# Building the attention diagonal from transposed r*k, with ScalarE, in the lead and the first block

## The chip, the core and the metric

One core of one Trainium2 chip runs the whole program. The metric is device microseconds (us) of one launch; the figure for a kernel is the median of its runs. Engines are named as in the profile: PE (TensorE matmul), PEld (its weight load), DVE (VectorE), ACT (ScalarE), POOL (GpSimd), SP (SyncE, which issues nearly all DMAs).

## The reference

```python
for t in range(768):                       # B=4, H=8, D=48, S=768
    cur = einsum('bhd,bhe->bhde', u * k[t], v[t])
    y[t] = einsum('bhd,bhde->bhe', r[t], state + cur)
    state = w * state + einsum('bhd,bhe->bhde', k[t], v[t])
x = y as (3072 tokens, 384)
h = x @ w_in;  x = (relu(h) ** 2) @ w_out         # layer 1, 384 -> 2048 -> 384
h = x @ w_in2; x = (h - tanh(h)) @ w_out2         # layer 2
```

A token's own term is a diagonal: (sum over d of r*u*k) times v. All other terms go through decays that are powers of w.

## The kernel before, in words

**Tiles.** 128 tokens of one batch are a tile `i`; tiles 0 to 3 are the first 128 tokens of the four batches, 4 to 7 the next 128, up to 23. Four tiles are a block `j` of 512 tokens. Each of the two dense layers runs as 16 units `f` per block: `gemm1` (9 matmuls of 512 columns, the products of high and low parts), an activation, `gemm2` (9 more).

**Lead.** The attention of tiles 0 to 3 stands before everything else, in `lead_*`. `rk` holds r and k with d on the partitions ("transposed"), `nat` holds r, k and v with tokens on the partitions ("natural"). `table_b` makes the powers of w by doubling (`vtab`, then `tk` and `tr`). `lead_a` multiplies transposed k and r by them, `lead_b` makes 128x128 scores on PE (`sc`). The diagonal comes from natural r: `lead_u` multiplies by u (POOL), `lead_r` by natural k, `lead_s` sums over d (DVE), `lead_d` spreads it over identity matrices `am`, half of them by POOL and half by ACT, and `lead_m` copies the scores of earlier tokens over them (DVE, four COPY_PREDICATED). `lead_k` decays natural k on POOL, with a table that `table_c` made by PE transposes. `lead_c` then makes y and the state on PE, and `lead_e` evacuates y as a high part (ACT) and a low part (DVE), and the state (ACT). `fill` puts dummy matmuls between, on PE.

**Later tiles** go through `att_*` in two halves of 64 tokens, while the dense units of the block before run. Tiles 4 to 7 run in units 0 to 11 of block 0 (called the first block here). `att_u`, `att_r`, `att_k` and both halves of `att_d` run on POOL, `att_s` (a sum), `att_a` (decays of r and k), `att_m` (predicated copy) and `decay` on DVE; `att_b`, `att_v`, `att_c` are PE matmuls; `put_state` copies the state into `vs` on ACT.

**Weights.** In the first block each unit's weights arrive as one 768 KB DMA into one of three buffers `raw` and are split: `conv0` (ACT), `conv1` (two DVE operations), `conv2` (ACT), `conv3` (POOL for units 0 to 2, DVE after), three units ahead of their matmuls. Then `raw` is free for the next DMA.

**Order.** The order is written out by hand at the end of the kernel: each engine runs its instructions in the order in which the calls stand there. A unit `n` of the first block runs `act1_low(n)`, `conv2` and `conv3(n+2)`, `front(n+1)` (its `gemm1` and activation), `conv1(n+3)`, any attention part, `gemm2_1(n)`, `conv0(n+4)`. One call sets the state of a tile's first half:

```python
def state_0(i):
    if TPB <= i < NTAU:
        s = st_m[i % TPB]
        put_state(i, 0, s)                 # ACT
        dec_t[i] = a2.tile([GP, NP, D], F32, tag="dec", name="dec")
        decay(dec_t[i], s)                 # DVE
```

Of the kernel before, what the change touches and what calls it, by code (L numbers as in the profile page):

```python
# [25 lines left out]
def decay_attention_moe_moe_kernel(  # L26
# [171 lines left out]
    def table_a():  # L198
        nc.sync.dma_start(out=vtab[:, :, 0], in_=w)

    def table_b():
# [18 lines left out]
        nc.vector.tensor_copy(tr[:, :, 0:64], tk[:, :, 127:63:-1])  # L220

    def table_c():
        kh = gp.tile([GP, NP, C], F32, tag="g", name="kh")
        nc.vector.tensor_tensor(
            kh[:, :, 0:127],
            vtab[:, :, 126::-1],
            vtab[:, :, 31:32].to_broadcast([GP, NP, 127]),
            op=ALU.mult,
        )
        nc.vector.tensor_copy(kh[:, :, 127:128], vtab[:, :, 31:32])  # L230
        pt = bank(7, "pt")
        for p in range(NP):
# [776 lines left out]
```

## Time and profile before

| | us |
|---|---|
| median of three runs | 926.96 |
| lowest and highest run | 926.81 and 927.23 |
| span of the profiled execution | 926.0 |
| PE busy | 896.6 (97%) |
| DVE busy | 638.8 (69%) |
| ACT busy | 631.8 (68%) |
| POOL busy | 255.1 (28%) |

The span runs from the first to the last instruction of the profiled execution; its own run time is not given apart, and the median is 0.96 us above its span. The lead takes the first 36 us, the first block ends at about 140 us, block 1 at about 223, layer 2 begins at about 530 and fills the rest. Busy shares over the whole span say little about the first 140 us, where the limits are others.

### The profile page before, as it was taken

Reading aid. Unit: us, or ns where it says so; the run is one execution under the profiler, and the core shown is the slowest. Engines: PE = TensorE matmul, PEld = TensorE weight load, DVE = VectorE, ACT = ScalarE, POOL = GpSimd, SP = SyncE. Lnnn points to the kernel's source line nnn. Section 1 sums busy time; section 2 is a strip of 40 time slices with the busy share of each in tenths; the row PEclk is TensorE's granted clock in tenths of the full one; section 3 lists DMA queues with packets and bytes.
Section 4 is the critical chain, followed back from the end, with each engine's and each line's share of the span. In section 5 each row is a group of like instructions: output and inputs, shape, how many; then the busy total and the mean of one; then the engine's idle time right before and its main releaser. Section 6 shows DMA issues by size and latency. Waiting matters only on the chain.

```text
span 926.0 us, 14869 instructions
## 1 busy us (share of the span) xinstructions
PE 896.6 (97%) x5688; PEld 731.8 (79%) x5688; DVE 638.8 (69%) x1016; ACT 631.8 (68%) x1121; POOL 255.1 (28%) x214
## 2 busy tenths in 40 slices
PE   6799989999999999999999999999999999999997
PEld 5687777887888788788888778888888888888885
DVE  8899971332242233123167799999999999999996
ACT  2756754444444444444588898888988988988985
POOL 4854423553555455453202011001001001010000
PEclk7989999999999999999999999999999999999999
DMA  8846711322131122210455100010100100100000
GB/s 234 223 151 196 221 55 43 92 55 81 52 99 51 56 79 56 79 53 8 176 199 210 65 27 12 7 52 11 57 8 6 57 12 1 57 12 1 34 1 35
DMA packets 32168, 67.73 MB, mean 73 GB/s; under 512 B 5600, under 2 KB 17888, under 8 KB 32096
## 3 DMA queue, kind: packets, MB, share of 16 engines
q1 hardware_dynamic: 31792, 66.48, 23.3%
q8 instruction: 45, 0.74, 0.3%
q10 hardware_dynamic: 304, 0.30, 0.2%
q14 instruction: 27, 0.22, 0.1%
HBM read 55.35 MB, written 9.44 MB: 70 GB/s over the span
## 4 chain that ended last, share of the span: by engine, by line
PE 83%; DVE 8%; ACT 4%; DMA 3%; issue 1%; SPq 0%; POOL 0%; ACTq 0%; DVEq 0%; POOLq 0%
PE h L579 37%; PE o L729 20%; PE acc L619 18%; PE y L413 2%; PE sc L351 2%; PE pv L362 2%; DVE ra L322 1%; DMA first_kv<-in_nat_dram 1%; DMA x2d<-x2s 1%; DVE w L107 1%; DMA raw<-in_w_dram 1%; DVE raw L92 1%; DVE raw L93 1%; DVE ra L372 1%; ACT x2s L635 1%
## 5 line engine op out<-in xcount | busy, mean ns | idle before, releaser
L579 PE MATMUL h<-xt,w 128*128 128x512 f32 x864 | 214.5, 394 | 0.0
L579 PE MATMUL h<-xs,w 128*128 128x512 f32 x864 | 211.4, 389 | 0.0
L579 PEld LDWEIGHTS h<-xt,w 128*128 128x128 f32 x864 | 164.6, 191 | 34.9
L579 PEld LDWEIGHTS h<-xs,w 128*128 128x128 f32 x864 | 162.2, 188 | 34.0
L593 ACT ACTIVATE g<-h 128x512 f32<-128x512 f32 x96 | 57.2, 596 | 153.9 <-PE h L579 153.8
L619 PE MATMUL acc<-ghi,w 128*128 128x512 f32 x576 | 156.0, 402 | 3.3 <-ACT x2s L635 3.3
L729 PE MATMUL o<-ghi,w 128*128 128x512 f32 x576 | 148.8, 390 | 0.3 <-ACT ghi L700 0.3
L599 POOL TENSOR_TENSOR glo<-g,ghi 128x512 fp32r<-128x512 f32 x64 | 82.5, 1289 | 167.8 <-ACT ghi L596 76.0
L619 PEld LDWEIGHTS acc<-ghi,w 128*128 128x128 f32 x576 | 105.5, 189 | 27.5 <-ACT x2s L635 5.0
L729 PEld LDWEIGHTS o<-ghi,w 128*128 128x128 f32 x576 | 107.6, 188 | 24.0 <-ACT ob L740 1.3
L652 POOL TENSOR_TENSOR xs<-x2f,xs 128x512 fp32r<-128x512 f32 x18 | 24.4, 1355 | 313.5 <-DVE xs L651 313.5
L432 DVE TENSOR_TENSOR ys<-y,ys 112x128 fp32r<-112x128 f32 x20 | 5.8, 289 | 134.6 <-ACT xt L430 134.6
L619 PE MATMUL acc<-glo,w 128*128 128x512 f32 x288 | 84.4, 395 | 6.6 <-DVE glo L608 6.6
L676 ACT ACTIVATE th<-h 128x512 f32<-128x512 f32 x96 | 57.5, 599 | 42.0 <-DVE hy L675 42.0
L729 PE MATMUL o<-glo,w 128*128 128x512 f32 x288 | 84.2, 394 | 1.9 <-DVE glo L706 1.9
L689 DVE SCALAR_TENSOR_TENSOR hy<-q,hy 128x512 f32<-128x512 f32 x96 | 78.2, 815 | 0.1
L675 DVE SCALAR_TENSOR_TENSOR hy<-h,y 128x512 f32<-128x512 f32 x96 | 66.0, 688 | 13.5 <-ACT y L673 13.4
L694 DVE COPY_PREDICATED hy<-mask,th 128x512 f32<-128x512 uint8 x96 | 70.8, 738 | 0.0
L679 DVE TENSOR_TENSOR th<-h,th 128x512 f32<-128x512 f32 x96 | 66.1, 689 | 5.9 <-ACT th L676 0.7
L619 PEld LDWEIGHTS acc<-glo,w 128*128 128x128 f32 x288 | 54.2, 189 | 20.2 <-DVE glo L608 8.7
L677 ACT ACTIVATE q<-y,ba 128x512 f32<-128x512 f32 x96 | 68.7, 716 | 0.0
L680 ACT ACTIVATE q<-y,bb 128x512 f32<-128x512 f32 x96 | 68.5, 713 | 0.0
(105 smaller groups left out, 1246.0 us busy)
## 6 DMA issues: line engine op xcount, KB each, us to landing
raw<-in_w_dram SPq DMA_DIRECT2D x32, 768.0 KB, 5.0
rkt<-in_rk_dram SPq DMA_DIRECT2D x20, 448.0 KB, 4.9
x2d<-x2s SPq DMA_DIRECT2D x18, 256.0 KB, 2.2
x2f<-x2d SPq DMA_DIRECT2D x18, 256.0 KB, 3.2
out_dram<-ob SPq DMA_DIRECT2D x18, 256.0 KB, 2.3
rnt<-in_nat_dram SPq DMA_DIRECT2D x20, 192.0 KB, 4.5
kn<-in_nat_dram SPq DMA_DIRECT2D x20, 192.0 KB, 4.7
...
```

The costliest lines, as they stand in the source:

```text
L579: nc.tensor.matmul(h, lhsT=w_in(layer, f, part, kk), rhs=x[:, xpart, kk, :], start=(n == 0), stop=(n == 3 * KK - 1),)
L593: nc.scalar.activation(out=g, in_=h, func=AF.Relu)
L599: nc.gpsimd.tensor_tensor(lo, g, hi.bitcast(F32), op=ALU.subtract)
L619: nc.tensor.matmul(acc[j][m], lhsT=w_out(1, f, part, m * 128, (m + 1) * 128), rhs=g, start=(f == 0 and n == 0), stop=(f == NF - 1 and n == 2),
L675: nc.vector.scalar_tensor_tensor(out=hy, in0=h, scalar=PK, in1=y, op0=ALU.mult, op1=ALU.mult)
L676: nc.scalar.activation(out=th, in_=h, func=AF.Tanh)
L677: nc.scalar.activation(out=q1, in_=y, func=AF.Square, bias=p2["ba"], scale=1.0)
L679: nc.vector.tensor_tensor(th, h, th, op=ALU.subtract)
L680: nc.scalar.activation(out=q2, in_=y, func=AF.Square, bias=p2["bb"], scale=1.0)
L689: nc.vector.scalar_tensor_tensor(out=hy, in0=q2, scalar=PD, in1=hy, op0=ALU.add, op1=ALU.mult)
L694: nc.vector.copy_predicated(hy, mask, th)
L729: nc.tensor.matmul(acc[j][m], lhsT=w_out(2, f, part, m * 128, (m + 1) * 128), rhs=g, start=(f == 0 and n == 0), stop=(f == NF - 1 and n == 2),
```

## The change

1. `first` and `load` no longer load natural r for tiles 0 to 7, nor natural k for tiles 0 to 3, nor u for the lead. Loads for tiles 4 and 5 move ahead of the third weight load.
2. `lead_a` makes r*k transposed (`pr`, DVE). `lead_p` multiplies it on PE with a column of u (four matmuls of 2 columns) and transposes the decayed k with four PE transposes, both into one bank; ACT copies the diagonal (`bt0`) and the natural k (`first_kn`) out, and makes all eight identity products `am` of a tile.
3. In the first block `att_a` overwrites transposed r with r*k (DVE), `att_v` makes the diagonal by 16 matmuls of one column, ACT copies it out, `att_d(i, 0)` stays on POOL and the other half is eight ACTIVATEs of 64x64 on ACT (`att_da`). `att_u`, `att_r`, `att_s` of tiles 4 to 7 are gone. `att_m` of these tiles moves one unit later, ahead of the next `att_a`.
4. Powers of w and 1/w are doubled together (`pw`); the state of a lead tile is now kept without a decay, so `state_0` of tiles 4 to 7 first multiplies it by w^96 on DVE.
5. `clear` (memsets on DVE) moves from the start into the lead, and `table_c` and `table_d` to its end.

```diff
+    wu = ac.tile([GP, 3 * NP], F32, name="wu")
+    ucol = wu[:, NP:3 * NP].rearrange("p (P a) -> p P a", a=2)
+    pw = ac.tile([GP, 2, NP, 65], F32, name="pw")
+    wdec = pw[:, 0, :, 64:65]
+    w96 = ac.tile([GP, NP, 1], F32, name="w96")
     tr = ac.tile([GP, NP, C], F32, name="tr")
-    tk = ac.tile([GP, NP, C], F32, name="tk")
+    tk = tr[:, :, 127::-1]
...
-        nc.sync.dma_start(out=rn_t[i].rearrange("p h d -> p (h d)"), in_=nat[i, :, 0])
-        if i == 0:
-            nc.scalar.dma_start(out=ub0, in_=u[0:1, :].to_broadcast([128, DM]))
-        nc.sync.dma_start(out=kv_t[i].rearrange("p x h d -> p x (h d)"), in_=nat[i, :, 1:3])
...
+        nc.sync.dma_start(out=v, in_=nat[i, :, 2])
...
-            nc.sync.dma_start(out=rn_t[i], in_=nat[i, :, 0])
+            if i >= 2 * TPB:
+                nc.sync.dma_start(out=rn_t[i], in_=nat[i, :, 0])
...
+        nc.vector.tensor_copy(pw[:, 0, :, 1], wu[:, 0:NP])
+        nc.vector.reciprocal(out=pw[:, 1, :, 1], in_=wu[:, 0:NP])
         m = 1
-        while m < C:
+        while m < 64:
             nc.vector.tensor_tensor(
+                flat2[:, :, 1 + m:1 + 2 * m], flat2[:, :, 1:1 + m],
+                flat2[:, :, m:m + 1].to_broadcast([GP, 2 * NP, m]), op=ALU.mult,
             )
             m *= 2
...
+    def table_c():
+        nc.vector.tensor_tensor(w96, pw[:, 0, :, 64:65], pw[:, 0, :, 32:33], op=ALU.mult)
+        kh = gp.tile([GP, NP, L], F32, tag="g", name="kh")
+        nc.vector.tensor_tensor(
+            kh, pw[:, 0, :, 63::-1], pw[:, 0, :, 32:33].to_broadcast([GP, NP, L]), op=ALU.mult,
+        )
         table.append(kh)
...
+    def att_da(i, a):
+        q = half(a)
+        for c in range(2):
+            for p in range(NP):
+                nc.scalar.activation(
+                    out=ra_t[i][q, a, p, c, :], in_=ident[q, q], func=AF.Copy, scale=bt_t[i][q, c, p:p + 1]
+                )
...
+        if i < 2 * TPB:
+            nc.vector.tensor_tensor(rk_t[i][:, 0], rk_t[i][:, 0], rk_t[i][:, 1], op=ALU.mult)
+        nc.vector.tensor_tensor(k, k, tab(tr[:, :, 95:31:-1], GP), op=ALU.mult)
...
+            if i < 2 * TPB:
+                nat_q.append(lambda: att_k(i, G))
+                return
...
+            bt = pb[:, 2 * GPS:2 * GPS + 2 * NP].rearrange("p (c P) -> p c P", c=2)
+            for c in range(2):
+                for p in range(NP):
+                    for a in range(2):
+                        q = slice(64 * a, 64 * a + D)
+                        nc.tensor.matmul(
+                            bt[half(a), c, p:p + 1], lhsT=rk_t[i][q, 0, p, c * L:(c + 1) * L],
+                            rhs=ucol[q, p, a:a + 1], start=True, stop=True,
+                        )
+            bt_t[i] = a2.tile([128, 2, NP], F32, tag="bt", name="bt")
+            nc.scalar.activation(out=bt_t[i], in_=bt, func=AF.Copy)
+            att_d(i, 0)
+            att_da(i, 1)
...
         if TPB <= i < NTAU:
             s = st_m[i % TPB]
+            if i < 2 * TPB:
+                nc.vector.tensor_tensor(s, s, w96.to_broadcast([GP, NP, D]), op=ALU.mult)
             put_state(i, 0, s)
...
+    def lead_a(i):
+        V = nc.vector
+        r, k = rk_t[i][:, 0], rk_t[i][:, 1]
+        V.tensor_tensor(pr_t[i], r, k, op=ALU.mult)
+        if i:
+            V.tensor_tensor(k, k, tk, op=ALU.mult)
+            V.tensor_tensor(r, r, tr, op=ALU.mult)
+            return
+        up, down = pw[:, 0, :, 0:64], pw[:, 1, :, 64:0:-1]
+        V.tensor_tensor(k[:, :, 0:64], k[:, :, 0:64], pw[:, 0, :, 63::-1], op=ALU.mult)
+        V.tensor_tensor(k[:, :, 64:C], k[:, :, 64:C], pw[:, 1, :, 1:65], op=ALU.mult)
+        V.tensor_tensor(r[:, :, 0:64], r[:, :, 0:64], down, op=ALU.mult)
+        V.tensor_tensor(r[:, :, 64:C], r[:, :, 64:C], up, op=ALU.mult)
...
+    def lead_p(i):
+        pk = bank(1, "pk")
+        for p in range(NP):
+            nc.tensor.matmul(
+                pk[:, NP * GP + 2 * p:NP * GP + 2 * p + 2], lhsT=pr_t[i][:, p, :], rhs=ucol[:, p, :],
+                start=True, stop=True,
+            )
+        for p in range(NP):
+            nc.tensor.transpose(pk[:, p * GP:(p + 1) * GP], rk_t[i][:, 1, p, :], ident[0:GP, 0:GP])
+        diag[i] = a2.tile([128, H], F32, tag="bt", name="bt0")
+        nc.scalar.activation(out=diag[i], in_=pk[:, NP * GP:NP * GP + H], func=AF.Copy)
+        lead_d(2 * i)
+        nc.scalar.activation(
+            out=kv_t[i][0], in_=pk[:, 0:NP * GP].rearrange("p (P x) -> p P x", x=GP), func=AF.Copy
+        )
+        lead_d(2 * i + 1)
...
+    def lead_d(d):
+        i, e = divmod(d, 2)
+        am_t[d] = gp.tile([128, 4, C], F32, tag="ghi", name="am", bufs=4)
+        for z in range(2):
+            for a in range(2):
+                h = 4 * e + 2 * z + a
+                nc.scalar.activation(
+                    out=am_t[d][:, 2 * a + z], in_=ident, func=AF.Copy, scale=diag[i][:, h:h + 1]
...
         table_a()
-        clear()
-        for i in range(TPB):
-            first(i)
-            if i == 2:
-                load_w(1, 0)
...
         lead_z(0)
         lead_z(1)
+        lead_zc(0)
+        lead_zc(1)
         table_b()
         lead_a(0)
-        lead_u(0, G)
-        lead_zc(0)
+        lead_p(0)
         lead_b(0)
         lead_b(1)
-        rs(0)
-        lead_d(0)
-        lead_zc(1)
-        table_c()
-        table_d()
-        lead_u(1, G)
         lead_a(1)
-        lead_k(0, G)
+        lead_p(1)
         fill(FILL[0])
         mb(0)
-        lead_u(2, G)
-        rs(1)
-        lead_d(1)
-        lead_k(1, G)
         lead_a(2)
...
-            fill(FILL[1][i])
+            pt = lead_c(i)
+            fill(FILL[1][i], pt)
             if i + 2 < TPB:
-                rs(i + 2)
+                lead_p(i + 2)
             if i + 1 < TPB:
                 mb(i + 1)
-            if i < 2:
-                load(i + 4)
             lead_e(i)
             if i + 2 < TPB:
                 lead_zc(i + 2)
-                lead_d(i + 2)
-                lead_k(i + 2, G)
-            if i + 3 <= TPB:
-                (lead_u if i + 3 < TPB else att_u)(i + 3, G)
             if i + 3 < TPB:
-                if i == 0:
-                    lead_r(3, G)
-                lead_a(i + 3, G)
+                lead_a(i + 3)
             if i == 0:
                 conv0(1, 0)
                 conv1(1, 0)
                 conv2(1, 0)
                 conv3(1, 0, G)
             if i == 1:
+                clear()
                 conv0(1, 1)
-                att_r(4, G)
             if i == 2:
                 conv1(1, 1)
             if i == 3:
                 conv2(1, 1)
                 conv3(1, 1, G)
+        table_c()
+        table_d()
...
+                if i2 <= 2 * TPB:
+                    att_m(i2 - 1)
...
-                att_m(i)
+                if i >= 2 * TPB:
+                    att_m(i)
```

**ACT in the lead, round tile 2** (`am`: identity products, `xt`: y of tile 0, `raw` and `w_0`: the first weights). Before:

```order
L559 ACTIVATE xt<-y 128x3x128
L563 ACTIVATE st<-pt 48x192 x2
L524 ACTIVATE vz<-first_kv 128x3x16 x2
L494 ACTIVATE am<-ident,bt_325 128x128 x4
L84 ACTIVATE raw<-raw 128x768
L101 ACTIVATE w_0_372<-raw 128x768
```

With the change:

```order
L494 ACTIVATE bt_329<-pk 128x8
L524 ACTIVATE am<-ident,bt_329 128x128 x4
L496 ACTIVATE first_kn<-pk 128x448
L524 ACTIVATE am<-ident,bt_329 128x128 x4
L586 ACTIVATE xt<-y 128x3x128
L588 ACTIVATE st<-pt 112x192
L84 ACTIVATE raw<-raw 128x768
L101 ACTIVATE w_0_370<-raw 128x768
L494 ACTIVATE bt_420<-pk 128x8
```

The evacuation of tile 0 (`xt`) now stands behind the whole diagonal of tile 2, and tile 3's diagonal behind the first weights' `conv2`.

**DVE in the lead, between tile 0's low part (L560 before, L587 now) and tile 3's predicated copy** (L506, L531). Before:

```order
L560 TENSOR_TENSOR xt<-y,xt 128x3x128
L461 TENSOR_TENSOR first<-first,tr 112x512
L92 TENSOR_SCALAR raw<-raw 128x768
L93 SCALAR_TENSOR_TENSOR raw<-raw 128x768
L482 TENSOR_REDUCE bt_414<-first 128x8
L506 COPY_PREDICATED am<-low,sc 128x256 x4
L560 TENSOR_TENSOR xt<-y,xt 128x3x128
L506 COPY_PREDICATED am<-low,sc 128x256 x4
```

With the change:

```order
L587 TENSOR_TENSOR xt<-y,xt 128x3x128
L471 TENSOR_TENSOR first<-first 112x512
L473 TENSOR_TENSOR first<-first,tr 112x512
L474 TENSOR_TENSOR first<-first,tr 112x512
L92 TENSOR_SCALAR raw<-raw 128x768
L93 SCALAR_TENSOR_TENSOR raw<-raw 128x768
L531 COPY_PREDICATED am<-low,sc 128x256 x4
L587 TENSOR_TENSOR xt<-y,xt 128x3x128
L179 MEMSET vs_97 32x400
...
L182 MEMSET ra_103 32x512
L531 COPY_PREDICATED am<-low,sc 128x256 x4
```

Two more multiplies and the eleven memsets of `clear` now stand ahead of tile 3's copy.

**ACT in the first block, units 1 to 3** (`vs<-st`: `put_state` of `state_0`; `w_4`, `w_6`: `conv2`; what an instruction waits for stands in brackets). Before:

```order
L382 ACTIVATE vs_101<-st 48x192 x2
L84 ACTIVATE raw<-raw 128x768 [waits DMAHW7_49,Pool_49]
L101 ACTIVATE w_4_698<-raw 128x768 [waits DVE_49]
...
L382 ACTIVATE vs_101<-s_838 48x192 [waits DVE_49]
L382 ACTIVATE vs_101<-s_838 48x192
L84 ACTIVATE raw<-raw 128x768 [waits DMAHW6_49]
L101 ACTIVATE w_6_849<-raw 128x768
```

With the change:

```order
L402 ACTIVATE vs_99<-st 48x192 [waits DVE_49]
L402 ACTIVATE vs_99<-st 48x192
L84 ACTIVATE raw<-raw 128x768 [waits DMAHW0_49,Pool_49]
L101 ACTIVATE w_4_737<-raw 128x768
...
L375 ACTIVATE bt<-pv 128x8 [waits PE_49]
L307 ACTIVATE ra_103<-ident,bt 64x64 [waits Activation_49]
L307 ACTIVATE ra_103<-ident,bt 64x64 x7
L402 ACTIVATE vs_99<-s_900 48x192 [waits DVE_49]
L402 ACTIVATE vs_99<-s_900 48x192
L84 ACTIVATE raw<-raw 128x768 [waits DMAHW6_49]
L101 ACTIVATE w_6_908<-raw 128x768
```

The first `put_state` now waits for DVE (the multiply by w^96) with `conv0` and `conv2` behind it, and nine instructions stand ahead of the second.

## Rows read from the trace of the kernel before

**Rows 1.** Windows: length, busy PE, PEld, DVE, ACT, POOL; PE clock, DMA share, GB/s.
```profile
0.00:36.00 36.00, 28.37 (x308) 23.50 (x308) 28.87 (x61) 15.45 (x44) 23.98 (x30) 0.81 0.94 249
...
36.30:62.30 26.00, 20.69 (x157) 16.86 (x156) 23.96 (x26) 16.27 (x28) 19.89 (x13) 0.80 0.51 162
62.30:80.20 17.90, 16.84 (x154) 13.21 (x152) 16.98 (x25) 13.17 (x24) 5.58 (x4) 1.00 0.63 196
...
142.00:223.00 81.00, 80.09 (x675) 65.53 (x674) 25.31 (x49) 38.44 (x75) 41.76 (x37) 1.00 0.24 68
```

**Rows 2.** Timeline: start, length, engine, line, instructions; DVE in the first block.
```profile
62.34 0.68 DVE L608 TENSOR_TENSOR glo<-g,ghi 128x512 fp32r<-128x512 f32 x1
...
95.77 1.38 DVE L322 TENSOR_TENSOR ra<-rkt,tr 48x512 f32<-48x512 f32 x2
...
117.80 0.68 DVE L608 TENSOR_TENSOR glo<-g,ghi 128x512 fp32r<-128x512 f32 x1
```

**Rows 3.** Timeline of the lead: PE.
```profile
14.84 0.98 PE L233 MATMUL pt<-ident,kh 112*128 112x112 f32 x4 [0.59 <-DVE kh L230]
...
15.75 1.09 PE L248 MATMUL pt<-ident,kh 48*64 48x48 f32 x16
...
18.59 2.08 PE L472 MATMUL sc<-first 48*128 48x128 f32 x16
...
20.60 0.70 PE L537 MATMUL y<-am,vz 128*64 128x128 f32 x4
...
23.91 1.05 PE L256 MATMUL warm<-low,zero 112*128 112x256 bf16 x8
...
36.38 4.35 PE L579 MATMUL h<-xt,w 128*128 128x512 f32 x18
```

**Rows 4.** Windows of the lead, columns as in rows 1: the granted clock.
```profile
9.50:10.50 1.00, 0.00 (x0) 0.00 (x0) 0.97 (x2) 0.00 (x0) 0.73 (x1) 0.75 0.96 224
...
12.00:20.60 8.60, 7.84 (x60) 6.21 (x60) 8.53 (x15) 3.60 (x13) 5.86 (x5) 0.50 1.04 296
...
23.50:24.00 0.50, 0.50 (x17) 0.45 (x14) 0.45 (x2) 0.48 (x1) 0.50 (x2) 0.84 1.11 432
```

**Rows 5.** DMA issues at 1.5 to 2 us: out, queue, count, KB, us to landing.
```profile
first<-in_rk_dram SPq DMA_DIRECT2D x1, 448.0 KB, 7.0
```

**Rows 6.** Timeline of the lead: ACT and DVE.
```profile
0.95 0.39 DVE L174 MEMSET vs<- 32x400 f32 x1 [0.95 <-PEq L992]
...
4.18 0.70 DVE L178 MEMSET st<- 32x768 f32 x1
...
13.20 1.28 ACT L494 ACTIVATE am<-ident,bt 128x128 f32<-128x128 f32 x4 [1.50 <-DVE bt L482]
...
25.30 0.55 DVE L92 TENSOR_SCALAR raw<-raw 128x768 uint32<-128x768 uint32 x1
...
32.60 1.44 DVE L506 COPY_PREDICATED am<-low,sc 128x256 f32<-128x256 uint32 x4 [1.74 <-POOL am L496]
...
35.76 0.49 ACT L559 ACTIVATE xt<-y 128x384 fp32r<-128x384 f32 x1 [1.67 <-PE y L541]
```

**Rows 7.** Timeline of ACT in the first block, and the DVE operation that waits for it.
```profile
58.25 0.72 ACT L382 ACTIVATE vs<-st 48x192 f32<-48x192 f32 x2
59.00 0.90 ACT L84 ACTIVATE raw<-raw 128x768 f32<-128x768 f32 x1
59.80 0.89 ACT L101 ACTIVATE w<-raw 128x768 fp32r<-128x768 f32 x1
60.59 0.59 ACT L593 ACTIVATE g<-h 128x512 f32<-128x512 f32 x1
...
62.41 0.26 ACT L430 ACTIVATE ys<-y 112x128 fp32r<-112x128 f32 x1
...
73.23 1.08 DVE L107 TENSOR_TENSOR w<-raw,w 128x768 fp32r<-128x768 f32 x1 [0.66 <-ACT w L101]
```

**Rows 8.** Groups of DVE from 36 to 120 us: busy us, mean ns.
```profile
L322 DVE TENSOR_TENSOR ra<-rkt,tr 48x512 f32<-48x512 f32 x10 | 13.3, 1332 | 0.1
```

More of the change, by code (lines that the diff above doesn't have):

```diff
@@ L198, in table_a, with warm_act @@
     def table_a():
-        nc.sync.dma_start(out=vtab[:, :, 0], in_=w)
+        nc.sync.dma_start(out=wu, in_=w)
+    def warm_act():
+        t = ac.tile([1, 1], F32, name="warm_act")
+        nc.vector.memset(t, 0.0)
+        nc.scalar.activation(out=t, in_=t, func=AF.Copy)
     def table_b():
+        flat2 = pw.rearrange("p x P e -> p (x P) e")
+        nc.vector.tensor_copy(pw[:, 0, :, 1], wu[:, 0:NP])
+        nc.vector.reciprocal(out=pw[:, 1, :, 1], in_=wu[:, 0:NP])
         m = 1
-        while m < C:
+        while m < 64:
@@ L217, in table_b @@
         nc.vector.tensor_tensor(
-            tk[:, :, 96:128], tk[:, :, 64:96], tk[:, :, 95:96].to_broadcast([GP, NP, 32]), op=ALU.mult
+            kh, pw[:, 0, :, 63::-1], pw[:, 0, :, 32:33].to_broadcast([GP, NP, L]), op=ALU.mult,
         )
[L220 to L232, printed above, removed]
-            nc.tensor.transpose(pt[:, p * GP:(p + 1) * GP], kh[:, p, :], ident[0:GP, 0:GP])
-        pv = pt[:, 0:NP * GP].rearrange("p (P x) -> p P x", x=GP)
-        tv = kt0.rearrange("p (P two) d -> p two P d", two=2)
-        nc.scalar.activation(out=tv[:, 0], in_=pv[:, :, 0:D], func=AF.Copy)
-        nc.scalar.activation(out=tv[:, 1], in_=pv[:, :, 64:GP], func=AF.Copy)
@@ L238, in table_c @@
         table.append(kh)
-    table = []
     def table_d():
@@ L248, in table_d, with fill @@
                 nc.tensor.matmul(
-                    pt[half(a), p * D:(p + 1) * D], lhsT=kh[q, p, L:C], rhs=ident[q, q], start=True, stop=True,
+                    pt[half(a), p * D:(p + 1) * D], lhsT=kh[q, p, :], rhs=ident[q, q], start=True, stop=True,
                 )
         nc.scalar.activation(out=kt_tab, in_=pt[:, 0:GPS], func=AF.Copy)
-    def fill(n, b=1):
-        t = bank(b, "warm")
+    def fill(n, t=None):
+        t = bank(2, "warm") if t is None else t
         for q in range(n):
             nc.tensor.matmul(
-                t[:, (q % 2) * 256:(q % 2 + 1) * 256], lhsT=zero, rhs=low[0:GP].bitcast(BF16), start=True, stop=True
+                t[:, 256:512], lhsT=zero, rhs=low[0:GP].bitcast(BF16), start=True, stop=True
             )
@@ L548, in lead_c @@
             a = h % 2
+            m = GP - 64 if a else 64
             nc.tensor.matmul(
[L550 removed]
+                pv[64 * a:64 * a + m, h // 2, :], lhsT=kn[:, h // 2, 64 * a:64 * a + m], rhs=vn[:, h, :],
+                start=True, stop=True,
             )
         lead_y[i] = (yv, pv)
+        return pt
     def lead_e(i):
@@ L560, in lead_e @@
         nc.vector.tensor_tensor(dst[:, 1], yv, dst[:, 0].bitcast(F32), op=ALU.subtract)
-        for a in range(2):
-            q = slice(64 * a, 64 * a + D)
-            nc.scalar.activation(out=st_m[i][q], in_=pv[q], func=AF.Copy)
+        nc.scalar.activation(out=st_m[i], in_=pv[0:GP], func=AF.Copy)
     hbank = {1: [3, 4], 2: [3, 4, 5]}
@@ L766, in decay_attention_moe_moe_kernel @@
         table_a()
-        clear()
-        for i in range(TPB):
-            first(i)
-            if i == 2:
-                load_w(1, 0)
+        first(0)
+        first(1)
+        warm_act()
+        nc.vector.memset(pw[:, :, :, 0:1], 1.0)
+        first_value(0)
+        load_w(1, 0)
+        first(2)
+        first_value(1)
+        first(3)
+        first_value(2)
+        first_value(3)
+        load_w(1, 1)
+        load(4)
+        load_w(1, 2)
+        load(5)
         for a in range(2):
-            nc.scalar.dma_start(out=ub[half(a)], in_=u[1:2, a * GPS:(a + 1) * GPS].to_broadcast([64, GPS]))
-        load_w(1, 1)
-        load_w(1, 2)
+            nc.scalar.dma_start(out=ub[half(a)], in_=u[:, a * GPS:(a + 1) * GPS].to_broadcast([64, GPS]))
         setup_pool()
```

108 lines of the change are left out of this document (32 added, 76 removed).

## The prediction

> **What bounds the kernel now.** I read the windows first, because the page's shares are means over unlike stages. From 142 to 223 us PE is busy for 80.1 of 81 us at clock 1.00 [rows 1], and the blocks after it look alike: from the end of the first block on PE sets the time, and the change touches nothing there. So whatever the change gains or loses must be gained or lost before about 140 us, and then passes to the end one to one. Two stages lie before that. In the lead (0 to 36 us) the DMA engines are busy 0.94 of the time, PE runs at a mean clock of 0.81 and no engine is full [rows 1]: it is a chain. In the first block DVE is the fullest engine, 24.0 of 26.0 us and then 17.0 of 17.9 us, while ACT has 16.3 and 13.2 [rows 1]. Its pace can be read from one line: the low part of unit 2 (L608) starts at 62.34 us, that of unit 11 at 117.80 [rows 2], so nine units took 55.5 us. PE's first dense matmul starts at 36.38 [rows 3]. I build the sum from these marks: front(0) at 36.38, low part 2 at 62.34, low part 11 at 117.80, end of the span 926.0. The median of the runs lies 0.96 above this span, and I carry that difference over.
>
> **Step 1, the lead up to the first y: earlier by 4.1 us.** Tile 0's transposed r and k landed 7.0 us after their issue at 1.6 [rows 5]. Without u beside them I take 7.5 (bounds 7.0, and 8.75 if the tables, not the load, are late). DVE then makes r*k, k and r. A 48x512 multiply costs 0.69 [rows 2], and operations that follow each other start a little closer, so 0.61 for r*k and four halves at 0.36: r is ready at 9.6. PE follows. Its clock is the question: in this trace the clock fell by 10.5 us after the first fills, stayed at 0.50 (1.2 of 2.4 GHz) from 12 to 20.6 although PE was busy 7.8 of these 8.6 us with small matmuls and fills, and rose only near 23.7, after three microseconds of the y matmuls [rows 4]. The new small matmuls are of the small kind, so I take 0.50: four 2-column matmuls 0.7, four transposes 0.8 (L233, 0.98 to their last end), two scores 1.8 (L472, 2.08), tile 1's matmuls 1.5, eight fills 1.7, two scores 1.8 [rows 3]. The first y matmul starts at 16.5 instead of 20.60 [rows 3].
>
> **Step 2, from there to front(0): later by 11.5 us, so 7.4 in sum.** The y matmuls take 3.3 (20.60 to the fills at 23.91 [rows 3]), the fills about 0.9 with the clock rising in them, tile 2's small matmuls 0.3: t = 21.0. Before, the evacuation of tile 0 followed its y at once. Now it stands behind tile 2's diagonal on ACT, and the rest is a relay, ACT to DVE to ACT:
> - diagonal out of PSUM 0.3, eight identity products 2 x 1.25 (four took 1.28 [rows 6]), natural k 0.5: t + 3.3;
> - y's high part 0.45 (0.49 [rows 6]), low part 0.5, three multiplies 1.85, `conv1` 1.45 (L92 0.55 [rows 6], its second operation about 0.96), `conv2` 0.85 (0.80 to the next start [rows 7]): t + 8.4;
> - tile 3's diagonal, behind `conv2`, 3.3; tile 1's y 0.95: t + 12.65;
> - `clear`: its eleven memsets lasted from 0.95 to 4.18 [rows 6], 3.2; tile 3's copy 1.43 (1.44 [rows 6]): t + 17.3;
> - tile 3's y 2.9. PE has had nothing for about 5 us here, and a shorter pause made it fall before [rows 4], so half clock; high and low part 1.05; w^96 and `kh` 0.55, which stand behind the low part; `table_d` 1.05 (1.09 [rows 3]): t + 22.8.
>
> front(0) starts at 43.8 instead of 36.38: **+7.4**. The saved DMA bytes don't help here: weights and tiles 4 and 5 land earlier, but nothing in this relay waits for them.
>
> **Step 3, front(0) to the low part of unit 2: 22.1 instead of 26.0 us, -3.9.** Here the change pays. Before, `att_a` of tile 4 ran into POOL: ten L322 took a mean of 1332 ns from 36 to 120 us [rows 8], where two take 1.38 us with POOL idle [rows 2]. `att_u`, `att_r` and half of `att_d` leave POOL, so I take the free durations. The path moves to ACT: h(0) at half clock 3.85, activation of unit 0 2.1, `conv2` 0.85, `put_state` 0.75, `conv0` 0.9, activation of unit 1 1.95, diagonal and eight 64x64 products 2.2, second `put_state` 0.7, `conv0` 0.9, `conv2` 0.9: 15.1. Then DVE: `conv3` 0.87, `conv1` 1.45, `att_m` 1.45, `att_a` 2.55 with the new r*k (0.62), w^96 and decay 0.7: 22.1. The 16 one-column matmuls hide, since PE waits for DVE here.
>
> The 64x64 products have no row. One is shorter than a 128x128 (four in 1.28) and longer than a 112x4 copy, so eight cost between 1.5 and 2.5; I take 2.0, nearer to the larger form, which has the same operands. The Trainium skill ("ScalarE: Activation LUTs", What ACT_TABLE_LOAD costs) gives 186 ns, 93 for each pointer operand and 0.833 per element, with 93 of overlap, which makes an estimate of 1.9 for the eight and would lower the sum by 0.3 over three tiles.
>
> **Step 4, low part 2 to low part 11: 60.9 instead of 55.5 us, +5.4.** These are three rounds of three units, each with one tile. DVE's own work changes little: r*k +0.62, w^96 +0.35, sum over d -0.46. But ACT gets two places at which it holds DVE up.
> (a) `state_0`. Before, `put_state` at 58.25 waited for nothing, `conv0` and `conv2` followed and were done at 60.6, and DVE's `conv3` came later [rows 7]. Now `put_state` waits for the multiply by w^96, which is behind `att_m` and `att_a` on DVE; `put_state` 0.77, `conv0` 0.88, `conv2` 0.87 follow while DVE has only decay and low part to do (0.95): DVE stands for 1.55.
> (b) The diagonal. Counted from the multiply, ACT has `conv2` done at 2.5, an activation (1.82 from 60.59 to 62.41 [rows 7]) 4.3, y 4.85, `conv0` and `conv2` 6.6, an activation 8.45, diagonal and products 10.75, `put_state`, `conv0`, `conv2` 13.2. DVE, which waited 0.66 for it before [rows 7], is there at 10.6 and stands for 2.65. Then `conv3` 0.87, `conv1` 1.45, `att_m` 1.45, `att_a` 2.55, w^96 0.35: a round of 19.9. With 0.3 for what is left of POOL two such rounds are 40.4; the third has no w^96 and no r*k for tile 8 but that tile's full POOL work, 20.5.
>
> **Sum.** 7.4 - 3.9 + 5.4 = +8.9; the 808.2 us after low part 11 are unchanged. 926.96 + 8.9 = 935.9, so **936**. Unknown costs: products +-0.5 a tile, tile 3's y at full clock -1.3, contention left 0 to 0.8 a round, first load and tables -0.5 to +1.2. By themselves they give 931 to 940.
>
> **The rivals.**
> *Full clock in the lead.* If the small matmuls come soon enough after the first fills to hold PE at 1.00, y of tile 0 starts near 13.5 and t is 17.0, held there by the landing of tile 2 behind the first weights. All else as above: 4.0 less, 932. For it: the pause is one microsecond instead of five. Against it: the same kind of work did not raise the clock in 8.6 us [rows 4].
>
> *The change pays: POOL off DVE's port, ACT ahead.* If ACT is ahead of DVE at (a) and (b), rounds cost DVE's work alone, 15.3 plus 1.2 of waits, so 16.5 against a mean of 18.5: -6. Step 3 gives -3.9, and the lead with the early clock and a warm tile 3 is late by only 1.9 (t = 17.0 gives 3.4, less 1.5): -8, of which I grant half, since the relay in the lead is written into the order: 923. It decides if `conv2` is done within 1 us of the w^96 multiply and before 10.6. For it: DVE is the fullest engine and loses contention [rows 1, 8]; before, ACT had 13.2 of 17.9 [rows 1]. Against it: (a) is an order on ACT, not a load. The Trainium skill ("SBUF — State Buffer", SBUF: two separate sides) says that GpSimd and VectorE share one port pair by an exclusive lock and that ScalarE waits for nobody; by that rule all that leaves POOL for ACT comes back to DVE, and the trace agrees as far as 1332 against 690 ns goes.
>
> *A draw.* The lead late by 7, rounds as in the last case: 926 to 928.
>
> *Worse.* DVE's standing still frees the `raw` buffers late, the next weights arrive late, and PE's pauses pass into half clock: one such round more is +3 to +5, 941.
>
> **How the numbers follow.** A measurement can tell about 0.2% (1.9 us) from no change. Forecast 0.47, full clock 0.20, worse 0.08: slower 0.75. The change pays: 0.18 faster. A draw: 0.07 same. The range from 923 to 941 leaves out the far half of "pays" and the far half of "worse"; the forecast's own range is 931 to 940.
>
> **What would show it.** Right: the first dense matmul at 40 to 46 us with ACT's chain before it; DVE's L107 idle for ACT over 1 us, twice a round; ACT's `put_state` waiting for DVE's L413; POOL's busy time in the first block halved and L321 near 690 ns; all blocks after unchanged. Wrong: front(0) before 37, or rounds under 17.5 us.

## The result, and the profile after

The changed kernel takes 938.83 us (median of four runs, 935.39 to 942.03) against 926.88 for the kernel before on the same chip: ratio 1.0131, 95% interval 1.0101 to 1.0162: slower, by 1.3%. The runs form two pairs, 935.4 and 935.9, 941.7 and 942.0; the profiled one is of the first pair (935.91, span 934.1). The tenth and eleventh experiment bear on what sets the pairs apart.

Windows of the lead, of front(0) to low part 2, of low part 2 to low part 11, and of 81 us in block 1 (columns as in [rows 1]):

```profile
0.00:41.50 41.50, 32.08 (x356) 27.27 (x356) 23.91 (x62) 20.31 (x56) 6.01 (x21) 0.91 0.61 184
41.55:64.15 22.60, 19.72 (x156) 16.07 (x156) 15.89 (x26) 13.74 (x29) 8.65 (x6) 0.79 0.44 143
64.15:128.12 63.97, 58.59 (x584) 46.95 (x584) 52.10 (x76) 47.61 (x100) 15.95 (x12) 0.92 0.51 163
151.00:232.00 81.00, 80.17 (x676) 65.57 (x675) 25.31 (x49) 38.29 (x74) 41.79 (x37) 1.00 0.23 67
```

Block 1 is as before [rows 1]. DMA share and POOL are well down in the lead and no engine is full there: it is still a chain. From low part 2 to low part 11 DVE works 52.1 us of 64.0.

The same stretch before, from 62.34 to 117.80, a view not shown ahead:

```profile
62.34:117.80 55.46, 50.55 (x454) 40.01 (x452) 52.32 (x74) 38.73 (x67) 23.54 (x15) 0.97 0.63 191
```

DVE's work is the same (52.3). So the 8.5 us are time in which DVE stands.

The lead, PE (the first y, tile 3's y, front(0); against [rows 3]), and ACT and DVE between them (against [rows 6]):

```profile
13.93 0.45 PE L561 MATMUL y<-am,vz 128*64 128x128 f32 x4
...
35.46 0.70 PE L561 MATMUL y<-am,vz 128*64 128x128 f32 x4 [3.96 <-DVE am L531]
...
41.55 5.55 PE L604 MATMUL h<-xt,w 128*128 128x512 f32 x18
```

```profile
18.21 0.18 ACT L494 ACTIVATE bt<-pk 128x8 f32<-128x8 f32 x1 [3.05 <-PE pk L492]
...
21.70 0.56 DVE L587 TENSOR_TENSOR xt<-y,xt 128x384 fp32r<-128x384 f32 x1 [5.80 <-ACT xt L586]
...
25.76 0.91 ACT L101 ACTIVATE w<-raw 128x768 fp32r<-128x768 f32 x1 [3.06 <-DVE raw L93]
...
30.05 0.56 DVE L587 TENSOR_TENSOR xt<-y,xt 128x384 fp32r<-128x384 f32 x1 [2.98 <-ACT xt L586]
...
33.88 1.43 DVE L531 COPY_PREDICATED am<-low,sc 128x256 f32<-128x256 uint32 x4
...
40.14 0.33 ACT L588 ACTIVATE st<-pt 112x192 f32<-112x192 f32 x1 [1.30 <-PE pt L249]
```

The brackets read as a relay: DVE stands 5.80 us for ACT, ACT 3.06 for DVE, DVE 2.98 for ACT, and PE 3.96 for DVE.

The first round of the block, ACT, DVE and PE (against [rows 2, 7]):

```profile
63.87 0.74 ACT L402 ACTIVATE vs<-st 48x192 f32<-48x192 f32 x2 [1.89 <-DVE st L413]
...
66.33 0.96 DVE L107 TENSOR_TENSOR w<-raw,w 128x768 fp32r<-128x768 f32 x1 [1.50 <-ACT w L101]
...
72.17 2.02 ACT L307 ACTIVATE ra<-ident,bt 64x64 f32<-64x64 f32 x8
72.19 1.14 PE L382 MATMUL pv<-vs,kn 64*64 64x48 f32 x32 [0.75 <-ACT bt L375]
...
73.44 0.35 DVE L421 TENSOR_TENSOR s<-dec,pv 112x192 f32<-112x192 f32 x1 [0.73 <-PE pv L382]
...
76.54 0.96 DVE L107 TENSOR_TENSOR w<-raw,w 128x768 fp32r<-128x768 f32 x1 [1.36 <-ACT w L101]
```

`put_state` (L402) waits 1.89 for the multiply by w^96 (L413) and DVE then 1.50 for the `conv2` behind it: that is (a). Ahead of the third `conv3` of the round DVE stands 1.36, that is (b), and 0.73 for PE's `pv`, which waits for ACT's copy of the small diagonal products out of the same PSUM tile: the prediction did not have this one. Groups of DVE from low part 2 to 11, columns as in [rows 8], of the kernel before and of the changed one (L107 is `conv3`, L421 the start of `state_1`, L321 part of `att_a`):

```profile
L107 DVE TENSOR_TENSOR w<-raw,w 128x768 fp32r<-128x768 f32 x9 | 9.3, 1030 | 2.4 <-ACT w L101 2.4
```
```profile
L107 DVE TENSOR_TENSOR w<-raw,w 128x768 fp32r<-128x768 f32 x9 | 9.2, 1023 | 7.9 <-ACT w L101 7.9
...
L321 DVE TENSOR_TENSOR ra<-rkt,tr 48x512 f32<-48x512 f32 x6 | 5.3, 890 | 0.0
...
L421 DVE TENSOR_TENSOR s<-dec,pv 112x192 f32<-112x192 f32 x3 | 1.1, 354 | 3.0 <-PE pv L382 3.0
```

5.5 more for ACT (L107) and 3.0 for PE (L421) make the 8.5.

### The profile page after: what moved, and what is told of

Read it like the earlier page. It is cut to its first block, busy times and chain, and to the rows that moved or that the text cites. A ratio compares the mean times of both kernels' runs of the same rounds, so it can differ in the third digit from the quotient of the medians.

```text
span 934.1 us, 15217 instructions
## 1 busy us (share of the span) xinstructions
PE 905.6 (97%) x5860; PEld 740.4 (79%) x5860; DVE 625.2 (67%) x1019; ACT 642.6 (69%) x1167; POOL 218.2 (23%) x194
## 3 DMA queue, kind: packets, MB, share of 16 engines
q1 hardware_dynamic: 30304, 64.12, 21.6%
## 4 chain that ended last, share of the span: by engine, by line
PE 83%; ACT 8%; DVE 6%; issue 1%; DMA 1%; POOL 0%; ACTq 0%; DVEq 0%; POOLq 0%
PE h L604 37%; PE o L754 20%; PE acc L644 18%; PE pv L382 2%; PE y L435 2%; PE sc L356 2%; ACT w L101 1%; ACT raw L84 1%; DMA x2d<-x2s 1%; ACT g L619 1%; PE warm L249 1%; DVE ra L321 1%; ACT am L524 1%; ACT g L618 1%; DVE ra L392 1%
## 5 line engine op out<-in xcount | busy, mean ns | idle before, releaser
L644 PE MATMUL acc<-ghi,w 128*128 128x512 f32 x576 | 158.0, 406 | 3.3 <-ACT x2s L660 3.3
L708 ACT ACTIVATE mask<-y,bm 128x512 uint8<-128x512 f32 x96 | 68.2, 710 | 0.0
```

Of the source, the lines that this page charges most:

```text
L644: nc.tensor.matmul(acc[j][m], lhsT=w_out(1, f, part, m * 128, (m + 1) * 128), rhs=g, start=(f == 0 and n == 0), stop=(f == NF - 1 and n == 2),
L708: nc.scalar.activation(out=mask, in_=y, func=AF.Sign, bias=p2["bm"], scale=1.0)
```

## The experiments

Marks of each profiled execution in us, and the times:

| | front(0) | low part 2 | low 2 to 11 | median us (runs) | ratio to before, 95% |
|---|---|---|---|---|---|
| before | 36.38 | 62.34 | 55.46 | 926.88 (4) | |
| changed | 41.55 | 64.15 | 63.97 | 938.83 (4) | 1.0131 (1.0101 to 1.0162) |
| 1 w^96 early | 41.48 | 64.45 | 57.73 | 930.42 (10) | 1.0044 (1.0027 to 1.0062) |
| 2 pv first | 43.80 | 67.96 | 64.25 | 940.35 (4) | 1.0147 (1.0114 to 1.0180) |
| 3 diagonal on POOL | 41.53 | 64.84 | 61.15 | 935.63 (4) | 1.0105 (1.0066 to 1.0145) |
| 4 diagonal later | 41.85 | 65.68 | 64.30 | 938.33 (4) | 1.0123 (1.0094 to 1.0151) |
| 5 clear earlier | 37.28 | 61.04 | 63.63 | 933.44 (4) | 1.0066 (1.0048 to 1.0084) |
| 6 lead's order | 35.25 | 57.55 | 62.26 | 927.70 (10) | 1.0012 (0.9995 to 1.0029) |
| 7 = 1, 2, 3 | 41.43 | 65.47 | 58.17 | 934.24 (4) | 1.0073 (1.0056 to 1.0090) |
| 8 = 7, 6, fills | 31.74 | 53.51 | 56.85 | 919.82 (4) | 0.9924 (0.9903 to 0.9945) |
| 9 = 1, 6, fills | 37.08 | 60.74 | 57.32 | 923.75 (6) | 0.9946 (0.9923 to 0.9969) |
| 10 gap filled | 41.24 | 65.53 | 62.04 | 935.61 (4) | 1.0092 (1.0074 to 1.0110) |
| 11 = 9, 10 | 32.33 | 54.93 | 57.04 | 920.45 (5) | 0.9924 (0.9909 to 0.9940) |

Each ratio is to the kernel before as it ran beside the variants on the same chip: 926.45 (13 runs) for 1 to 4, 927.76 (13) for 5 to 8, 927.83 (10) for 9 to 11. Three variants (5, 6, 10) leave the block as the change has it; with the changed kernel their stretches run from 62.0 to 64.0, so less than 2 us there is not told apart.

**1, the multiply by w^96 early.**
```diff
-            if i < 2 * TPB:
-                nc.vector.tensor_tensor(s, s, w96.to_broadcast([GP, NP, D]), op=ALU.mult)
...
         table_d()
+        nc.vector.tensor_tensor(st_all, st_all, w96[:, None].to_broadcast([GP, TPB, NP, D]), op=ALU.mult)
```


> Marks of the changed kernel: low part of unit 2 at 64.15, of unit 11 at 128.12 us, 64.0 between them (20.3, 21.6 and 22.0); DVE stands 1.50, 1.49 and 1.48 us before its first conv3 of each round, for ACT's conv2. My theory: these come from put_state waiting on DVE for w^96. One multiply of all four states at the end of the lead takes that wait away: the three stands go below 0.3, two multiplies of 0.35 leave the rounds, and low part 2 to low part 11 falls to 58.5 to 60.0 (-4 to -5.5). The time falls by 4 to 6 us. Rival, ACT full rather than held (it works without a gap from 63.9 to 76.5): what is gained before the first conv3 comes back as a longer stand before the third one, and the stretch stays above 62.5. Rival, POOL's use of the shared port sets the rounds: stretch unchanged within 0.7.

```profile
61.89 0.72 ACT L402 ACTIVATE vs<-st 48x192 f32<-48x192 f32 x2
...
65.05 0.95 DVE L107 TENSOR_TENSOR w<-raw,w 128x768 fp32r<-128x768 f32 x1
```

`put_state` waits for nothing now and DVE finds `conv2` done, in all three rounds. The stretch fell by 6.2, a little more than expected; PE's clock in it is 1.00 (0.92 before the edit). Of the 6.2, 4.8 are DVE's idle time and 1.4 its own work. From profile to profile the time fell by 6.1 (934.1 to 928.0). The stand before the third `conv3` stayed at 1.36, it did not grow. Both rivals fall: (a) is the order.

**2, pv ahead of the small products.** In `att_v` the loop that makes `pv` moves ahead of the loop that makes `bt`.

> In the changed kernel PE's att_v products (into pv) stand 0.75 and 1.53 us for ACT's copy of the small diagonal products out of the same PSUM tile, and DVE then stands 0.73, 1.54 and 0.72 us for pv before state_1, a wait that was not in my prediction. Here PE makes pv first and the 16 x 2 one-column products behind it. Theory, a new wait (PE held by ACT): DVE's three stands for pv go below 0.2, PE's clock in the second round rises from 0.84 towards 1.00, ACT's waits of 1.20 and 3.40 for h shrink, and the stretch from low part 2 to 11 falls from 64.0 to 61 to 62.5 (-1.5 to -3). Rival, ACT's order alone sets the rounds: in the first round ACT works without a gap, so the 0.73 moves to the stand before conv3 (1.36 to 2.1), and the stretch falls by less than 1.0. Time -0 to -1 by the rival, -1.5 to -3 by the theory.

```profile
L107 DVE TENSOR_TENSOR w<-raw,w 128x768 fp32r<-128x768 f32 x9 | 9.0, 999 | 10.5 <-ACT w L101 10.5
...
L421 DVE TENSOR_TENSOR s<-dec,pv 112x192 f32<-112x192 f32 x3 | 1.1, 351 | 0.8 <-ACT bt L384 0.8
```

The stands for `pv` went from 3.0 to 0.8, those for `conv2` from 7.9 to 10.5, and the stretch did not move. The theory of a new wait falls: the wait for `pv` is ACT's chain seen from another place.

**3, both halves of the diagonal on POOL.**
```diff
-            att_da(i, 1)
+            att_d(i, 1)
```


> Both halves of the first block's diagonal are made by POOL again, as before the change; the eight 64x64 products leave ACT (2.0 us a tile). Theory, ACT's products stand ahead of conv2: the stands before the third conv3 of a round (1.36, 1.15, 0.19) go below 0.3, a second POOL product of 1.0 to 1.4 us costs DVE up to 0.7 a round through slower operations, and low part 2 to 11 comes to 62.0 to 63.5 (64.0 now); front(0) to low part 2 goes from 22.6 to 20.5 to 21.5. Rival, POOL's share of the port is what counts in these rounds: they get longer, stretch 65 to 67. Rival, products are hidden by other waits: within 0.5 of 64.0.

The first round's third `conv3`, 1.36 in the changed kernel:

```profile
77.00 0.96 DVE L107 TENSOR_TENSOR w<-raw,w 128x768 fp32r<-128x768 f32 x1 [0.32 <-ACT w L101]
```

The three stands before the third `conv3` came to 0.32, 0.34 and 0.68, the stretch to 61.15, below what was expected: ACT's products are the (b) that was named. The stretch alone says less, since it lies only 0.9 under the lowest of an unchanged block. DVE's own work did not grow with POOL's second half: it fell from 52.1 to 50.9, with 1.5 us more of POOL. Front(0) to low part 2 was a miss, 23.3 instead of about 21. The reason stands in PE's and POOL's rows of that stage:

```profile
50.16 2.65 POOL L278 TENSOR_TENSOR kn<-kn,kt_tab 128x384 f32<-128x384 f32 x2
51.91 1.94 PE L382 MATMUL pv<-vs,kn 64*64 64x48 f32 x32 [2.82 <-POOL kn L278]
53.97 0.35 DVE L421 TENSOR_TENSOR s<-dec,pv 112x192 f32<-112x192 f32 x1 [2.97 <-PE pv L382]
```

There DVE waits for PE and PE for POOL's decay of natural k (`att_k`), not for ACT.

**4, the same diagonal one conv2 later.** `att_v` leaves `bt` in PSUM; ACT's copy, its eight products and POOL's half are called behind `conv2(1, f + 2)` of the next unit. `pv` is first, as in 2.

> Two edits: PE makes pv first, as in the second run, and ACT's copy of the diagonal with its eight products (and POOL's half) stands one conv2 later: behind the next unit's conv2 instead of ahead of put_state, conv0 and that conv2. No work is taken away. Theory, the order on ACT is what costs at (b): DVE's stands before the third conv3 of a round (1.36, 1.15, 0.19) go below 0.3; the products now run while DVE does conv3 and conv1 (2.4 us), and att_m may stand up to 0.5 for them. With the gain of pv first, low part 2 to 11 comes to 59.5 to 61.5 (64.0 now). Rival, ACT is full: the 2.2 us of diagonal only move into the next unit's activation, h is taken later, and the stretch stays at that of the run with pv first, within 0.7.

64.30, the same as 2, as the rival has it, but not by its reason. All stands for `conv2` fell from 10.5 to 8.1 us, but those before the third `conv3` were 1.12, 1.12 and 0.67 and not below 0.3. What was gained went into stands for `pv` (1.5 instead of 0.8) and into DVE's own work, 53.7 instead of 52.1: the products now run beside `conv1`, POOL's half among them, and L92 takes 844 ns instead of 556. So this order trades a wait for ACT against POOL's company.

**5, the memsets earlier.** `clear()` moves from `i == 1` to ahead of `lead_e(0)`.

> The changed kernel's eleven memsets (30.72 to 33.84 us, between the low part of tile 1's y and tile 3's predicated copy on DVE) move to where DVE stands idle for 5.8 us ahead of the low part of tile 0. Theory, the lead is a relay in which the memsets stand on the path: tile 3's copy starts at about 30.7 instead of 33.9, front(0) at 38.4 instead of 41.55 us (-3.1), and, if PE keeps its clock over the shorter pause, at 37.1; with a lead at half clock 2.3 more. Everything behind front(0) moves along: time -3 to -4. Rival, another late input takes over (ACT, a DMA): front(0) changes by less than 1 us.

```profile
33.46 0.45 PE L561 MATMUL y<-am,vz 128*64 128x128 f32 x4 [0.60 <-DVE am L531]
```

PE's pause before tile 3's y is 0.60 instead of 3.96, its clock stays 1.00 there, and front(0) comes at 37.28, 4.3 earlier: the memsets were on the path, and the half clock behind the pause of 3.96 is not there behind 0.60. The span fell by 3.4 (934.1 to 930.7), as expected.

**6, ACT's order in the lead.** Nothing is added or removed; `lead_x` holds the two ACT copies of `lead_e`, and the later calls of both are without them.
```diff
             fill(FILL[1][i], pt)
+            lead_x(i)
+            if i == 0:
+                conv0(1, 0)
             if i + 2 < TPB:
                 lead_p(i + 2)
```


> Only ACT's order in the lead changes: the copy-out of a tile's y and state stands ahead of the diagonal of the tile after the next, and the first weights' conv0 too. No instruction is added or removed. Theory, the relay ACT to DVE to ACT through the first weights' conv0, conv1 and conv2 holds the lead: conv1 of unit 0 starts near 19 instead of 24.1, the diagonal of tile 3 is ready near 28.6 with PE's sixteen fills ahead of it, the memsets run in that shadow, tile 3's y starts near 30 instead of 35.5, and front(0) at 35.5 to 37 (41.55 now; 2.3 more with a half clock lead). Rival, ACT has too much work there: the diagonals only move, front(0) above 40. Time -5 to -6 by the theory, 0 to -1.5 by the rival.

```profile
21.93 0.97 DVE L93 SCALAR_TENSOR_TENSOR raw<-raw 128x768 uint32<-128x768 uint32 x1
...
31.07 0.45 PE L561 MATMUL y<-am,vz 128*64 128x128 f32 x4 [0.19 <-DVE am L531]
```

Front(0) at 35.25, with a lead in which the clock was at 0.50 from 12 to 18 us. `conv1` ran at 21.3 to 22.9 rather than 19 (PE was late), but the memsets fitted in, and the whole lead's loss is gone by order alone. The span fell by 8.2 (934.1 to 925.9), more than the 5 to 6 expected; 1.7 of it lies in the stretch, where less than 2 is not told apart. Within the error the kernel equals the one before.

**7, the three edits of the block together.**

> In the first block three edits together: the four states multiplied by w^96 once in the lead, both halves of the diagonal on POOL, PE's pv ahead of the one-column products. Alone they brought the stretch from low part 2 to low part 11 from 64.0 to 57.7, 61.2 and 64.3 us. Theory, ACT's chain holds DVE at (a) and (b): with both gone, the 1.36 and 1.37 us of DVE's stands for conv2 and the 0.7 to 1.9 for pv that were left with the first edit go below 0.4, DVE's own work (50.7) plus 2 to 4 of stands remains: 53 to 55.5, that is what the kernel before had (55.5) or a little less. If the gains don't add because something else (weights' DMAs, h) is late next: 56.5 to 58. Rival, POOL's port: 58 or more. front(0) stays at 41.5. Time 926 to 929.

```profile
65.47:123.64 58.17, 54.66 (x589) 44.20 (x587) 54.00 (x74) 42.17 (x74) 20.28 (x15) 1.00 0.58 179
```
```profile
L93 DVE SCALAR_TENSOR_TENSOR raw<-raw 128x768 uint32<-128x768 uint32 x9 | 10.1, 1120 | 0.3
L107 DVE TENSOR_TENSOR w<-raw,w 128x768 fp32r<-128x768 f32 x9 | 9.1, 1016 | 1.0 <-ACT w L101 1.0
...
L419 DVE TENSOR_TENSOR s<-dec,pv 112x192 f32<-112x192 f32 x3 | 1.1, 352 | 2.3 <-ACT bt L384 2.3
```

The stands before `conv3` went to 1.0 in all, as expected. Those before `state_1` were 2.3 in all, 1.89 of it in the first round and not below 0.4, now put down to ACT's copy `bt`. The stretch is 58.17, no better than with edit 1 alone, and the time, 934.24, missed the 926 to 929. DVE works 54.0 us instead of 50.7: POOL is busy for 20.3 instead of 14.2, and L93 takes 1120 ns instead of 960. Here the rival has its part: with ACT's holds nearly gone, POOL's work lengthens DVE's. DVE's idle time fell by 2.9 against edit 1 and its work rose by 3.3: what was saved on ACT came back on DVE. In 3 it did not, so it depends on which operations meet.

**8, block, lead and fewer fills.** 7 and 6 together, and `FILL = (8, (8, 4, 4, 4))`.

> The three edits of the block, the lead's order on ACT, and 4 instead of 16 fills behind tile 1's y. Theory: the lead was late by its order and the block by ACT's two holds, both mended: front(0) at 34 to 36 us (36.4 before the change), low part 2 at 57 to 59, low part 11 at 111 to 113.5 (117.8 before), time 919.5 to 923, faster than both kernels. If fewer fills let PE's clock fall, front(0) is later by 2 to 3 and the time 922 to 925. Rival, the gains in the lead are lost behind it (weights or tiles 4 and 5 late for an earlier front(0)): low part 2 stays above 62 and the time at 925 to 928.

Earlier than expected at each mark (31.74, 53.51, 110.36) and 919.82 us: faster than both kernels.

**9, changes of place alone.** 1 and 6 and the fewer fills of 8; the eight products stay on ACT. Strictly, twelve dummy matmuls are gone and one multiply by w^96 stands for four; what the fewer fills give was not measured by itself.

> The changed kernel with its work as it is (eight products on ACT, pv behind the one-column products) and three changes of place alone: the states' multiply by w^96 in the lead, ACT's order in the lead, 4 instead of 16 fills behind tile 1's y. Theory, the loss was order and not the work moved to ACT: front(0) at 31.5 to 33.5 us, low part 2 at 53.5 to 56, low part 11 at 111 to 114 (117.8 before the change), time 919.5 to 923.5, faster than the kernel before. Rival, ACT's products cost too: DVE's stands for the third conv2 of a round stay at 1.3 as with the first edit alone, the stretch is 58 to 60, low part 11 at 114.5 or later, and the time 924 or more.

The median, 923.75, lies at the edge between the two, and the stands at (b) stayed (1.36 and 1.37), as the rival says. The stretch, 57.32, is below the rival's 58. But in this profile the lead is at half clock, which neither reckoned with; the fastest of the six runs took 918.52.

**10 and 11, PE's pause filled.** Eight `fill` behind `lead_b(1)`, in the changed kernel (10) and in 9 (11); e9 and e10 in the texts are the experiments 9 and 10.

> The changed kernel with eight more fills on PE, behind tile 0's scores and ahead of tile 1's small matmuls, where PE stands 0.93 us for ACT (its copy of natural k out of the one bank). Theory, the two groups of times of the changed kernel (935.4, 935.9 and 941.7, 942.0) are the lead with and without a fall of PE's clock behind this pause (in the profiles of other variants it was 0.50 from about 12 to 16 or 19 us, in the changed kernel's own 1.00 throughout): with the pause filled the clock stays 1.00 to the y of tile 1, the first y starts at 13.8 to 14.2, and the runs lie within 934 to 938. Rival, the spread comes from later pauses (4 us ahead of tile 3's y) or the first block: times still reach from 935 to 942.

> The three changes of place of e9 and the eight fills of e10. Theory: as e9, with the first y at 13.8 to 14.2 in each run; the runs lie within 3 us of each other, median 919 to 922. Rival, the extra fills cost what they give (the relay is held by ACT, not PE): the median is that of e9 within 1 us and so is its spread.

PE in the lead of 9, and in that of 11:

```profile
11.13 1.77 PE L485 MATMUL pk<-wu,first 112*128 112x2 f32 x8 [0.98 <-ACT first_kn L494]
...
17.39 0.70 PE L559 MATMUL y<-am,vz 128*64 128x128 f32 x4
```
```profile
10.09 1.05 PE L249 MATMUL warm<-low,zero 112*128 112x256 bf16 x8
11.14 1.05 PE L485 MATMUL pk<-wu,first 112*128 112x2 f32 x8
...
14.53 0.45 PE L559 MATMUL y<-am,vz 128*64 128x128 f32 x4
```

Windows from 12 to 14 us of 9 and of 11:

```profile
12.00:14.00 2.00, 2.00 (x12) 1.84 (x12) 1.97 (x4) 0.43 (x3) 0.38 (x1) 0.50 1.03 267
```
```profile
12.00:14.00 2.00, 2.00 (x24) 1.72 (x25) 1.22 (x3) 1.55 (x6) 0.00 (x0) 1.00 1.03 261
```

With the pause the clock in 9 was down to 0.50 (1.2 of 2.4 GHz) and y came at 17.39; filled, 14.53 at 1.00. All runs of 10 lie within 935.46 to 937.22 and all of 11 within 919.41 to 921.59. So I read the changed kernel's second pair, 6 us longer, as the lead at half clock: its mean granted clock is lower too (0.979 and 0.982 against 0.985 and 0.987), and between the profiles of 9 and 11 the end differs by 6.2 (924.2, 918.0). This is argued, not shown. A profile of that pair was not taken, and 2, whose lead has the changed kernel's order and ran at half clock, ends only 4.0 later than the changed kernel's profile (938.1, 934.1) with the same mean clock, 0.985. 11 has the change's work, the three changes of 9 and eight dummies, and is faster than both kernels; 8, with the products on POOL, cannot be told from it.

## Why the prediction was right, by its steps

Verdict, time and range held (936.0 against 938.83, and against 935.9 in the profiled run). The steps held less well than the sum. That they come to +8.1 against +8.9 is luck, since -2.6 and -2.2 stand against +3.1, +0.5 and +0.3. That the profiled run then met 935.9 to the decimal is luck again: its time lies 1.8 above its span (935.91, 934.1), where I had carried over 0.96.

| | forecast | profiled run |
|---|---|---|
| 1, first y | -4.1 | -6.7 |
| 2, to front(0) | +11.5 | +11.8 |
| 3, to low part 2 | -3.9 | -3.4 |
| 4, to low part 11 | +5.4 | +8.5 |
| behind it | 0 | -2.2 |
| sum | +8.9 | +8.1 |

**Step 1: two terms failed, PE at 0.50 and the load.** I took the clock of [rows 4] over. PE's chain to the first y took 6.9 instead of 8.3, with 0.93 of pause in it, and it began at 7.04 instead of 8.2, because the load came at 6.23, earlier than 7.5. PE was at 1.00 when it came, directly behind the fills, and stayed there in this run; y at 13.93. Where it fell in other variants, it fell near 12 us, not from the start. My rival "full clock in the lead" (0.20) is what the profiled run shows, but it was priced at 4.0 and front(0) came 2.25 ahead of the forecast's 43.8.

**Step 2: right in each link.** Counted from the end of tile 2's small matmuls (t = 18.2, forecast 21.0), `conv2` was done at t + 8.5 (forecast 8.4), tile 1's y at 12.4 (12.65), tile 3's copy at 17.1 (17.3), front(0) at 23.4 (22.8). The 0.6 is ACT's wait of 1.30 for the fills, which now write into the state's bank. Edits 5 and 6 show the two causes, memsets and ACT's order, each by itself.

**Step 3: right, with one link missing.** ACT's `conv2` was done 15.3 after front(0) (forecast 15.1), and DVE took 7.3 from there (7.0). But ACT's second `put_state` stood 1.08 for DVE, DVE for PE's `pv` and PE for POOL's `att_k`, as in experiment 3; the terms ahead of it were too long by about as much:

```profile
51.93 1.94 PE L382 MATMUL pv<-vs,kn 64*64 64x48 f32 x32 [2.88 <-POOL kn L278]
53.99 0.35 DVE L421 TENSOR_TENSOR s<-dec,pv 112x192 f32<-112x192 f32 x1 [2.97 <-PE pv L382]
54.38 0.74 ACT L402 ACTIVATE vs<-s 48x192 f32<-48x192 f32 x2 [1.08 <-DVE s L421]
```

The eight products took 2.02, where I had 2.0 and the Trainium skill's figures ("ScalarE: Activation LUTs", What ACT_TABLE_LOAD costs) an estimate of 1.9.

**Step 4: right in mechanism, one term too small.** (a) 1.55 forecast, 1.50, 1.49, 1.48 measured. (b) 2.65 forecast; stands for `pv` and `conv2` together 2.1, 2.7 and 0.9. That makes 10.9 with the second `conv3`s, where I had 12.6. What failed is "with 0.3 for what is left of POOL": of the 60.9 some 48 were DVE's work, and it was 52.1. Two of the signs named for POOL failed with it: POOL's work in this stretch fell from 23.54 to 15.95, not to half, and L321 took 890 ns, not near 690. The rounds took 20.3, 21.6 and 22.0 against 20.2, 20.2 and 20.5. In the first two the new r*k met POOL (1.38 and 1.40 instead of 0.69); the third alone has 19.09 of DVE's work, because tile 8's full POOL work falls into it:

```profile
118.54 1.54 DVE L107 TENSOR_TENSOR w<-raw,w 128x768 fp32r<-128x768 f32 x1 [0.19 <-ACT w L101]
120.01 1.42 DVE L92 TENSOR_SCALAR raw<-raw 128x768 uint32<-128x768 uint32 x1
...
123.86 2.64 DVE L321 TENSOR_TENSOR ra<-rkt,tr 48x512 f32<-48x512 f32 x2
```

I had named that work and mis-sized it.

**"Unchanged" behind low part 11 was wrong by 2.2.** Unit 12's `gemm1` before, and now:

```profile
118.53 1.07 PE L619 MATMUL acc<-glo,w 128*128 128x512 f32 x3 [3.49 <-DVE glo L608]
119.39 3.74 PE L579 MATMUL h<-xt,w 128*128 128x512 f32 x9
```
```profile
128.85 0.97 PE L644 MATMUL acc<-glo,w 128*128 128x512 f32 x3 [0.90 <-DVE glo L633]
129.66 2.21 PE L604 MATMUL h<-xt,w 128*128 128x512 f32 x9
```

Before, PE came out of a pause of 3.49 us and ran at half clock, 1.5 us longer. The other 0.7 I did not trace.

**"The change pays" (0.18) was the right picture of what it lacked.** Its condition, ACT ahead at (a) and (b), was not met; edit 1 meets it at (a), edit 6 in the lead, and 8 and 11 reach 920, below its 923. Its 15.3 of DVE's work a round was too low: the forecast's own round less its two stands (19.9 less 4.2) gives 15.7, and 17.4 was measured. It cited the Trainium skill's rule on the port pair of GpSimd and VectorE ("SBUF — State Buffer", SBUF: two separate sides). The runs bear out in part that work on POOL comes back to DVE: in experiment 7, 6.1 us more of POOL went with 3.3 more of DVE, in experiment 3, 1.5 more of POOL with 1.2 less of DVE.
